# Last output tile in three pieces, a row pitch of 160 bytes, and a new order of two weight differences, in a fused attention and max-out kernel

## Chip, cores, metric

One core of a Trainium2 chip. The metric is the device time of one execution in microseconds (us); the kernel before takes 183.31 us (median of 4 runs, 183.17 to 183.59). "Span" is the profile's time from the first to the last instruction; it is some 2 us shorter than the run's time.

## The reference

Batch 4, 8 heads, 768 tokens, head width 64, cut into 8 blocks of 96 tokens. Five rounds of row and column normalisation of an 8x8 matrix per head give P; P mixes the blocks of k and v; attention stays within a block; then a max-out layer follows.

```python
k_sorted = einsum('bhij,bhjcd->bhicd', P, k_b); v_sorted = the same with v_b
attn = softmax(scale * q_b @ k_sorted^T);  x = attn @ v_sorted       # (3072, 512)
out = maximum(x @ w1, x @ w2) @ w_out                                # d_ff = 1024
```

## The kernel before

The order of issue is made by hand; tiles and their semaphores are looked after by a tile framework. max(h1, h2) is computed as relu(x(W1-W2)) plus x W2, so W1 is overwritten by W1-W2 in four quarters (`w_difference`; quarters 1 to 3 on DVE), and W2 W_out is computed once (`w2_transposes`, `w_product`). PSUM is a pool of four tiles of 128 x 1024 fp32 values.

```python
v_sb = big.tile([BLK, 128, D + 2], BF16, ...)        # sorted v, rows of 66 bf16; column 64 is ones

def values(b, u):                                     # 32 units of 8 products
    ...
    for h2 in range(2):
        for ii in range(4):
            nc.tensor.matmul(ps[:, h2*512 + ii*65 : h2*512 + (ii+1)*65], e[...],
                v_sb[:, m0 + (hp + 4*h2)*8 + ih*4 + ii, 0:65], start=True, stop=True)
    # DVE: reciprocal of the ones column's sum (rs), then the product x

def moe_out_last(ti, pieces):                         # tiles 4 and 5 of the last batch
    for n0, n1, engines in pieces:
        ps = ps_f32("out_ps")
        out_products(ps[:, 0 : n1-n0], B-1, ti, n0, n1)        # 12 products
        w = (n1 - n0) // len(engines)
        for m, eng in enumerate(engines):
            o = opool.tile([128, w], FP32, tag=f"o{n0}{m}", name="o", bufs=1)
            ...   # copy by ACT ("A") or DVE ("D"), then a store from ACT's or SP's queue
# calls: moe_out_last(4, [(0, 512, "D")]);  moe_out_last(5, [(0, 256, "A"), (256, 512, "AD")])

# batch 0, near 30 us:
    w_difference(1)
    moe_h_products(0, 0, 1, (0, 2))                   # first half of hidden unit 1
    w2_out = w2_transposes(0, "D")
    moe_h(0, 0, 0, "A", (1, 3))
    w2_out()                                          # DVE copies w2T
    SC[5]()
# then: VA[4], w_difference(2); rest of hidden unit 1; SC[6], SC[7], VA[5], w_difference(3); hidden 2 ...

# loads during batch 0, step 8:
    pair_q(1, 0), pair_q(1, 1), load_q(2), load_v(2), load_v(3)
```

The softmax here doesn't subtract the row's maximum and nothing guards it: scores larger than these inputs give would overflow.

Of the kernel before, what the change touches and what calls it, by code (L numbers as in the profile page):

```python
# [10 lines left out]
FP32 = mybir.dt.float32  # L11
BF16 = mybir.dt.bfloat16
# [3 lines left out]
def kernel(  # L16
# [16 lines left out]
    nc = tc.nc  # L33
# [4 lines left out]
    B, H, S, D = q.shape  # L38
    NB = sort_net.shape[-1]
    BLK = S // NB  # L40
# [14 lines left out]
    big = ctx.enter_context(tc.tile_pool(name="big", bufs=1))  # L55
# [4 lines left out]
    opool = ctx.enter_context(tc.tile_pool(name="opool", bufs=3))  # L60
# [4 lines left out]
    def ps_f32(name):  # L65
        return psum.tile([128, 1024], FP32, tag="ps", name=name)

    def ps_bf16(name):
        return psum.tile([128, 2048], BF16, tag="ps", name=name)
# [21 lines left out]
    def pick(a_ns, d_ns):  # L91
        if load["A"] + a_ns <= load["D"] + d_ns:
            load["A"] += a_ns
            return "A"
        load["D"] += d_ns
        return "D"

    def evac(out_ap, in_ap, n, two_x=False, eng=None):
        a_ns, d_ns = (200 + n) / 1.2, (130 + (n / 2 if two_x else n)) / 0.96
        if eng:  # L100
            load[eng] += a_ns if eng == "A" else d_ns
        if (eng or pick(a_ns, d_ns)) == "A":
            nc.scalar.copy(out=out_ap, in_=in_ap)  # L103
        else:
            nc.vector.tensor_copy(out=out_ap, in_=in_ap)  # L105
# [82 lines left out]
    def w_difference(t, eng=None):  # L188
        n = DFF // 4
        (eng or nc.vector).tensor_tensor(  # L190
            out=w1_sb[:, :, t * n : (t + 1) * n],
            in0=w1_sb[:, :, t * n : (t + 1) * n],
            in1=w2_sb[:, :, t * n : (t + 1) * n],
            op=ALU.subtract,
        )
        if not eng:
            load["D"] += 600
# [66 lines left out]
    def selections(b):  # L264
        src = ident[0:G, b * 8 : b * 8 + 8]
        if b % 2 == 0:
            sel_v[b] = const.tile([G, 16, NB], BF16, tag=f"sel_v{b}", name="sel_v")
            nc.vector.tensor_copy(
                out=sel_v[b], in_=ident[0:G, b * 8 : b * 8 + 16].to_broadcast([G, 16, NB])
            )  # L270
        sel_k[b] = const.tile([G, 8, 16], BF16, tag=f"sel_k{b}", name="sel_k")
        nc.vector.tensor_copy(out=sel_k[b], in_=src.to_broadcast([G, 8, 16]))
# [40 lines left out]
                bd_v[b] = bd_v[b + 1] = bd.rearrange("p m i -> p (m i)")  # L313


    v_sb = big.tile([BLK, 128, D + 2], BF16, tag="v_sb", name="v_sb")
    nc.vector.memset(v_sb[:, :, D : D + 1], 1.0)
    xT = big.tile([128, 2, 2, 2, 2, TCH], BF16, tag="xT", name="xT")

# [194 lines left out]
    def w2_transposes(t, eng):  # L514
        ps = ps_bf16("tw_ps")
        for n in range(16):
            fb, dmt = t * 4 + n // 4, n % 4
            nc.tensor.matmul(
                ps[:, n * 128 : (n + 1) * 128],
                w2_sb[:, dmt, fb * 128 : (fb + 1) * 128],  # L520
                ident,
                is_transpose=True,
                start=True,
                stop=True,
            )
        return lambda: evac(
            w2T[:, t * 4 : t * 4 + 4, :].rearrange("p f d -> p (f d)"),
            ps,
            2048,
            two_x=True,  # L530
            eng=eng,
        )
# [38 lines left out]
    def moe_h(b, ch, t, eng=None, hps=(0, 2, 1, 3), n=0):  # L571
        moe_h_products(b, ch, t, hps, n)
        ps = h_ps[t]
        g = gpool.tile([128, 2, TCH], BF16, tag="g", name="g")
        src = ps.rearrange("p (t f) -> p t f", t=2)[:, :, 0:TCH]
        if (eng or pick((200 + 2 * TCH) / 1.2, (130 + 2 * TCH) / 0.96)) == "A":
            nc.scalar.activation(out=g, in_=src, func=AF.Relu)  # L577
        else:
            nc.vector.tensor_scalar(  # L579
                out=g, in0=src, scalar1=0.0, scalar2=None, op0=ALU.max  # L580
            )
        g_tiles[b, ch, t] = g
# [32 lines left out]
    def moe_out_last(ti, pieces):  # L615

        tok0 = (B - 1) * S + ti * 128
        for n0, n1, engines in pieces:
            ps = ps_f32("out_ps")
            out_products(ps[:, 0 : n1 - n0], B - 1, ti, n0, n1)  # L620
            w = (n1 - n0) // len(engines)
            for m, eng in enumerate(engines):
                o = opool.tile([128, w], FP32, tag=f"o{n0}{m}", name="o", bufs=1)
                src = ps[:, m * w : (m + 1) * w]
                if eng == "A":
                    nc.scalar.copy(out=o, in_=src)
                else:
                    nc.vector.tensor_copy(out=o, in_=src)
                (nc.scalar if eng == "A" else nc.sync).dma_start(
                    out=out[tok0 : tok0 + 128, n0 + m * w : n0 + (m + 1) * w], in_=o  # L630
                )


    def att(b):
# [24 lines left out]
    SC, VA, TR = att(0)  # L659
# [22 lines left out]
    moe_h_products(0, 0, 1, (0, 2))  # L682
    for b in range(1, B):
        selections(b)
    w2_out = w2_transposes(0, "D")
    moe_h(0, 0, 0, "A", (1, 3))
    w2_out()
    SC[5]()

    def turn(rows, c0):  # L690
        turn_v(rows, "D", c0, c0 + 24)
        load["D"] += 1600

    def load_rest():
# [1 line left out]
        load_k(2)  # L696

    tail = {
        0: [VA[4], lambda: w_difference(2)],
        1: [SC[6], SC[7], VA[5], lambda: w_difference(3)],  # L700
        2: [VA[6], TR[2], VA[7]],
        3: [TR[3], lambda: w2_transposes(1, "A")(), load_rest, lambda: block_diagonals(1)],
        4: [lambda: block_diagonals(2), lambda: turn(second, 0)],
# [11 lines left out]
    for b in range(B):  # L715
        units = [lambda t=t: moe_h(b, 0, t, None if b else "A") for t in range(4)]
        if b == 0:
            units[0] = lambda: None
            units[1] = lambda: moe_h(0, 0, 1, "A", (1, 3))
        units += [lambda t=t: moe_h(b, 1, t) for t in range(4)]  # L720
        cost = [1.3] * 8
        if b == 0:
            units += [lambda dmt=dmt: w_product(dmt) for dmt in range(4)]
            cost += [1.7] * 4
        units += [
            lambda ti=ti, part=part: moe_out(b, ti, part)
            for ti in range(6 if b < B - 1 else 4)
            for part in range(2)
        ]
        cost += [1.3] * 12  # L730
        if b == B - 1:
            units += [
                lambda: moe_out_last(4, [(0, 512, "D")]),
                lambda: moe_out_last(5, [(0, 256, "A"), (256, 512, "AD")]),
            ]
        steps, lo = [], 2
        if b < B - 1:
            qs = [lambda half=half: q_transposes(b + 1, half) for half in range(2)]
            pairs = [lambda two=two: pair_q(b + 1, two) for two in range(2)]
            ks = [lambda t=t, b=b: sort_k(b + 1, t) for t in range(3)]  # L740
            SC, VA, TR = att(b + 1)

            def group(*fs):
                return [lambda: [f() for f in fs]]

            if b == 0:
                lo = 9
                tail[7] += ks
                vs = [lambda t=t: sort_v(1, t) for t in range(4)]
                for m, c in enumerate((0, 24, 48, 72)):  # L750
                    VA[m + 1 : m + 2] = group(VA[m + 1], lambda c=c: turn(both, c))
                steps = group(*vs[:3]) + qs[:1] + group(*SC[0:2], vs[3]) + qs[1:] + VA[:1]
                steps += group(*SC[2:5]) + VA[1:2]
            elif b == 1:
                vs = [lambda t=t: sort_v_pair(2, t) for t in range(8)]
                steps = group(*pairs) + group(*ks) + qs[:1] + group(*SC[0:2], vs[0]) + qs[1:]
                steps += group(*vs[1:4]) + group(*vs[4:7]) + group(*SC[2:4], vs[7]) + VA[:2]
            else:
                steps = group(*pairs) + group(*ks) + qs + group(*SC[0:2])
                steps += group(*SC[2:5]) + VA[:2]  # L760
            rest = SC[4:] if b == 1 else SC[5:]
            steps += VA[2:3] + TR[:1] + VA[3:4]
            steps += group(*rest[:-1]) + TR[1:2] + VA[4:5] + rest[-1:] + VA[5:6]
        done = 0
        for n, unit in enumerate(units):
            unit()
            for step in tail.get(n, []):
                step()
            total = sum(cost[lo:-2])
            want = -(-len(steps) * sum(cost[lo : n + 1]) // total)  # L770
            while done < min(want, len(steps)):
                steps[done]()
                done += 1
        tail = {0: [VA[6]], 1: [TR[2], VA[7]], 2: [TR[3]]}
        if b == 0:
            tail[3] = [lambda: load_k(3)]
            tail[8] = [lambda: load_q(3)]
# [28 lines left out]
```

## Time and profile before

| | before |
|---|---|
| time, median | 183.31 us |
| span of the profiled run (itself 182.86 us) | 180.8 us |
| TensorE busy | 169.9 us (94%) |
| last product's end | 176.64 us |
| span's end after that | 4.18 us |

Times in views are us from the span's start. A timeline row has start, length, engine, source line, operation, output and input; in brackets stands how long the engine had been idle and what ended that. A wait row is "who and what, waited for whom: us in total, times, longest". The busy time of TensorE in one unit of values is overlapped, so its real cost is read from the chain of waits, where each piece lasts until the next begins. In the kernel before:

```profile
146.12 0.26 PE o_ps L463 x8
150.27 0.26 PE o_ps L463 x8
```

### The profile page before, as it was taken

What the parts mean: (1) busy time and instruction counts of PE and PEld (TensorE: products, weight loads), DVE (VectorE), ACT (ScalarE), POOL (GpSimd) and SP (SyncE); (2) the same over time, 40 slices, a digit from 0 to 9 for tenths busy, and PEclk for the clock granted to TensorE, in tenths of its full rate; (3) what the DMA queues carried; (4) which work ended last, traced back from release to release, by engine and by line L of the source; (5) the groups of instructions that cost most, each with busy time, mean ns of one, the idle gap of its engine ahead of it and who ended that gap; (6) DMA issues with size and microseconds to landing.
All of it is one profiled execution on the core that took longest, in us unless ns stands there. A gap on an engine that the chain in (4) does not pass through costs nothing.

```text
span 180.8 us, 4625 instructions
## 1 busy us (share of the span) xinstructions
PE 169.9 (94%) x2071; PEld 100.7 (56%) x2071; DVE 93.9 (52%) x192; ACT 92.0 (51%) x110; POOL 22.9 (13%) x39
## 2 busy tenths in 40 slices
PE   7698999999999999999989999999999999999990
PEld 2246666656655544577655554667555456554460
DVE  5878495759863595164587343446344427222010
ACT  3696776777665445277783341575815213530011
POOL 7941533200280000001000000000000000000000
PEclk9999999999999999999999999999999999999999
DMA  4999999999199992037400302300003032000341
GB/s 71 198 201 205 201 207 218 198 204 211 23 133 218 208 251 96 30 120 107 71 4 0 120 0 116 120 0 5 0 4 116 0 120 116 0 4 0 116 172 60
DMA packets 13939, 19.17 MB, mean 106 GB/s; under 512 B 800, under 2 KB 8864, under 8 KB 13920
## 3 DMA queue, kind: packets, MB, share of 16 engines
q0 software_dynamic: 10304, 12.58, 41.2%
q1 hardware_dynamic: 3328, 6.10, 8.8%
q8 instruction: 16, 0.26, 0.6%
q10 hardware_dynamic: 288, 0.20, 0.3%
q14 instruction: 3, 0.02, 0.0%
HBM read 25.17 MB, written 6.29 MB: 174 GB/s over the span
## 4 chain that ended last, share of the span: by engine, by line
PE 61%; DMA 22%; DVE 6%; issue 4%; POOL 3%; ACT 1%; ACTq 0%; POOLq 0%; DVEq 0%
PE out_ps L590 30%; PE h_ps L563 17%; DMA q_raw<-in_q_dram 15%; DMA v_raw<-in_v_dram 6%; PE o_ps L463 3%; PE tx_ps L495 3%; PE s_ps L438 2%; DVE x L480 2%; PE k_ps L371 2%; DVE g L579 2%; PE tq_ps L341 1%; PE v_ps L392 1%; POOL v_raw L153 1%; DMA out_dram<-o 1%; DVE xT L105 1%
## 5 line engine op out<-in xcount | busy, mean ns | idle before, releaser
L590 PE MATMUL out_ps<-wo_sb,g 128*128 128x512 bf16 (+1 forms) x200 | 47.9, 371 | 0.2 <-DVE g L579 0.2
L563 PE MATMUL h_ps<-xT,w_sb 128*128 128x384 bf16 x256 | 46.3, 326 | 0.6 <-DVE g L579 0.2
L563 PEld LDWEIGHTS <-w_sb 128*128 128x128 bf16 x256 | 23.6, 98 | 15.2 <-issue 0.5
L577 ACT ACTIVATE g<-h_ps 128x768 bf16<-128x768 f32 x24 | 19.5, 811 | 23.6 <-PE h_ps L563 23.6
L446 ACT ACTIVATE e<-s_ps 96x768 bf16<-96x768 f32 x32 | 24.1, 803 | 13.7 <-PE s_ps L438 13.6
L590 PEld LDWEIGHTS <-g 128*128 128x128 bf16 x200 | 17.5, 97 | 15.8 <-issue 0.2
L590 PE MATMUL out_ps<-wc,xT 128*128 128x512 bf16 (+1 forms) x100 | 24.8, 370 | 0.0
L103 ACT COPY o<-out_ps 128x1024 f32<-128x1024 f32 x8 | 8.1, 1013 | 31.1 <-PE out_ps L590 27.4
L480 DVE TENSOR_TENSOR x<-o_ps,rs 96x512 bf16<-96x512 f32 x32 | 22.0, 687 | 1.1
L474 DVE RECIPROCAL rs<-o_ps 96x8 f32<-96x8 f32 x32 | 6.4, 200 | 27.3 <-PE o_ps L463 27.2
L590 PEld LDWEIGHTS <-xT 128*128 128x128 bf16 x100 | 9.8, 98 | 11.0
L463 PEld LDWEIGHTS <-e 96*128 96x128 bf16 x256 | 11.5, 98 | 6.1 <-DVE x L480 0.7
L209 DVE COPY v_dc<-v_raw 64x1536 bf16<-64x1536 bf16 (+2 forms) x9 | 14.1, 1584 | 1.4 <-DMA v_raw<-in_v_dram 1.4
L579 DVE TENSOR_SCALAR g<-h_ps 128x768 bf16<-128x768 f32 x8 | 7.7, 958 | 13.5 <-PE h_ps L563 10.6
L463 PE MATMUL o_ps<-v_sb,e 96*128 96x65 bf16 x256 | 13.3, 194 | 1.0 <-DVE w2T L105 0.4
L105 DVE CAST v_sb<-v_ps 96x1024 bf16<-96x1024 f32 x7 | 8.5, 1218 | 5.9 <-PE v_ps L392 3.9
L103 ACT CAST v_sb<-v_ps 96x1024 bf16<-96x1024 f32 x9 | 8.7, 1018 | 3.3 <-PE v_ps L392 2.5
L103 ACT CAST kT<-k_ps 128x1024 bf16<-128x1024 f32 x10 | 9.5, 1024 | 0.0
L103 ACT COPY xT<-tx_ps 128x768 bf16<-128x768 bf16 x11 | 8.8, 797 | 1.5 <-PE tx_ps L495 1.5
L438 PEld LDWEIGHTS <-kT 64*128 64x128 bf16 x256 | 6.1, 94 | 5.5 <-issue 4.6
L129 POOL DMA_DIRECT2D q_raw<-in_q_dram x4 | 3.6, 900 | 43.3 <-DVE q_pair L326 41.0
L495 PEld LDWEIGHTS <-x 96*128 96x128 bf16 x128 | 6.8, 97 | 3.7 <-DVE x L480 1.7
(78 smaller groups left out, 163.9 us busy)
## 6 DMA issues: line engine op xcount, KB each, us to landing
out_dram<-o SPq DMA_DIRECT2D x11, 512.0 KB, 2.8
k_raw<-in_k_dram POOLq DMA_DIRECT2D x12, 256.0 KB, 13.4
q_raw<-in_q_dram POOLq DMA_DIRECT2D x4, 768.0 KB, 8.8
v_raw<-in_v_dram POOLq DMA_DIRECT2D x6, 384.0 KB, 11.6
w_sb<-in_moe_w_dram POOLq DMA_DIRECT2D x3, 512.0 KB, 16.1
wo_sb<-in_moe_w_out_dram POOLq DMA_DIRECT2D x2, 512.0 KB, 20.0
v_raw<-in_v_dram POOLq DMA_DIRECT2D x3, 256.0 KB, 4.5
w_sb<-in_moe_w_dram POOLq DMA_DIRECT2D x2, 256.0 KB, 14.1
```

Of the source, the lines that this page charges most:

```text
L103: nc.scalar.copy(out=out_ap, in_=in_ap)
L105: nc.vector.tensor_copy(out=out_ap, in_=in_ap)
L209: nc.vector.tensor_copy(out=dst, in_=src)
L438: nc.tensor.matmul(ps[:, h2 * 512 + ii * BLK : h2 * 512 + (ii + 1) * BLK], kT[b][rows, (hp * 8 + i) * BLK : (hp * 8 + i) * BLK + 128], rhs ...
L446: nc.scalar.activation(out=e[:, 0 : 8 * BLK].rearrange("p (t f) -> p t f", t=2), in_=ps[0:BLK].rearrange("p (t f) -> p t f", t=2)[:, :, 0 ...
L463: nc.tensor.matmul(ps[:, h2 * 512 + ii * 65 : h2 * 512 + (ii + 1) * 65], e[:, (h2 * 4 + ii) * BLK : (h2 * 4 + ii) * BLK + 128], v_sb[:, m0 ...
L480: nc.vector.tensor_tensor(out=x, in0=ov[:, :, :, 0:D], in1=rs.to_broadcast([BLK, 2, 4, D]), op=ALU.mult,)
L495: nc.tensor.matmul(ps[:, h2 * 1024 + ii * BLK : h2 * 1024 + (ii + 1) * BLK], x[:, h2, ii].rearrange("p n d -> p (n d)"), ident[0:BLK, 0:BL ...
L563: nc.tensor.matmul(h_ps[t][:, m * 512 : m * 512 + TCH], w1_sb[:, hp, fb * 128 : (fb + 1) * 128], xT[:, b % 2, ch, hp % 2, hp // 2, :], sta ...
L577: nc.scalar.activation(out=g, in_=src, func=AF.Relu)
L579: nc.vector.tensor_scalar(out=g, in0=src, scalar1=0.0, scalar2=None, op0=ALU.max)
L590: nc.tensor.matmul(dst, g_tiles[b, ch, m // 2][:, m % 2, off : off + 128] if m < NFB else xT[:, b % 2, ch, hp % 2, hp // 2, off : off + 12 ...
```

## The change

Intent: let the last stores leave sooner, put the rows of v_sb on multiples of 32 bytes, and fill DVE's idle times near 30 us so that TensorE doesn't wait there.

```diff
-    v_sb = big.tile([BLK, 128, D + 2], BF16, tag="v_sb", name="v_sb")
+    v_sb = big.tile([BLK, 128, D + 16], BF16, tag="v_sb", name="v_sb")
 ...
-            w = (n1 - n0) // len(engines)
-            for m, eng in enumerate(engines):
-                o = opool.tile([128, w], FP32, tag=f"o{n0}{m}", name="o", bufs=1)
+            o = opool.tile([128, n1 - n0], FP32, tag=f"o{ti}{n0}", name="o", bufs=1)
 ...   (copy and store as before, one engine per piece)
+    w_difference(2)
     w2_out = w2_transposes(0, "D")
     moe_h(0, 0, 0, "A", (1, 3))
     w2_out()
+    w_difference(3)
+    moe_h(0, 0, 1, "A", (1, 3))
     SC[5]()
 ...   (the three are taken out of their later places)
-                lambda: moe_out_last(5, [(0, 256, "A"), (256, 512, "AD")]),
+                lambda: moe_out_last(5, [(0, 256, "A"), (256, 384, "D"), (384, 512, "A")]),
```

More of the change, by code (lines that the diff above doesn't have):

```diff
@@ L617, in moe_out_last @@
         tok0 = (B - 1) * S + ti * 128
-        for n0, n1, engines in pieces:
+        for n0, n1, eng in pieces:
             ps = ps_f32("out_ps")
             out_products(ps[:, 0 : n1 - n0], B - 1, ti, n0, n1)
-            w = (n1 - n0) // len(engines)
-            for m, eng in enumerate(engines):
-                o = opool.tile([128, w], FP32, tag=f"o{n0}{m}", name="o", bufs=1)
-                src = ps[:, m * w : (m + 1) * w]
-                if eng == "A":
-                    nc.scalar.copy(out=o, in_=src)
-                else:
-                    nc.vector.tensor_copy(out=o, in_=src)
-                (nc.scalar if eng == "A" else nc.sync).dma_start(
-                    out=out[tok0 : tok0 + 128, n0 + m * w : n0 + (m + 1) * w], in_=o
-                )
+            o = opool.tile([128, n1 - n0], FP32, tag=f"o{ti}{n0}", name="o", bufs=1)
+            if eng == "A":
+                nc.scalar.copy(out=o, in_=ps[:, 0 : n1 - n0])
+            else:
+                nc.vector.tensor_copy(out=o, in_=ps[:, 0 : n1 - n0])
+            (nc.scalar if eng == "A" else nc.sync).dma_start(
+                out=out[tok0 : tok0 + 128, n0:n1], in_=o
+            )
     def att(b):
@@ L698 @@
     tail = {
-        0: [VA[4], lambda: w_difference(2)],
-        1: [SC[6], SC[7], VA[5], lambda: w_difference(3)],
+        0: [VA[4]],
+        1: [SC[6], SC[7], VA[5]],
         2: [VA[6], TR[2], VA[7]],
@@ L718 @@
             units[0] = lambda: None
-            units[1] = lambda: moe_h(0, 0, 1, "A", (1, 3))
+            units[1] = lambda: None
         units += [lambda t=t: moe_h(b, 1, t) for t in range(4)]
```

## The prediction

> **What bounds the kernel now.** I read the page first. Its table of busy time and its slices say that TensorE is the engine to watch, at full granted clock from end to end, and that the last slice is the one stretch where it stands still.
>
> ```profile
> PE 169.9 (94%) x2071; PEld 100.7 (56%) x2071; DVE 93.9 (52%) x192; ACT 92.0 (51%) x110; POOL 22.9 (13%) x39
> ...
> PE   7698999999999999999989999999999999999990
> ```
>
> So a change pays where it shortens TensorE's own list of work, one of its waits, or the stretch after its last product. I looked at those three in turn. The end first: the timeline of the last microseconds.
>
> ```profile
> 174.06 0.69 DVE L628 COPY o<-out_ps 128x512 f32<-128x512 f32 x1 [6.49 <-PE out_ps L590]
> ...
> 174.78 3.91 SPq L629 DMA_DIRECT2D out_dram<-o  x2
> ...
> 175.17 1.04 PE L590 MATMUL out_ps<-wo_sb,g 128*128 128x256 bf16 x8
> ...
> 176.04 0.60 PE L590 MATMUL out_ps<-wc,xT 128*128 128x256 bf16 x4
> 176.90 0.37 ACT L626 COPY o<-out_ps 128x256 f32<-128x256 f32 x1 [4.38 <-DMA out_dram<-o]
> 177.31 0.37 ACTq L629 DMA_DIRECT2D out_dram<-o  x1
> 177.72 0.27 ACT L626 COPY o<-out_ps 128x128 f32<-128x128 f32 x1 [0.45 <-ACT o L626]
> 178.02 0.34 ACTq L629 DMA_DIRECT2D out_dram<-o  x1
> 178.02 0.29 DVE L628 COPY o<-out_ps 128x128 f32<-128x128 f32 x1 [3.27 <-ACT o L626]
> ```
>
> The products are through at 176.64, but the span ends at 180.82: 4.18 us without a product. Three pieces queue in it. The copy of the first piece could have begun at 175.33, when its twelve products end, yet it waits to 176.90 for a transfer. The code says which: tile 4 and the first piece of tile 5 share one SBUF tag, so ACT must wait until the store of tile 4 has landed. Then ACT makes two copies with an issue between, and DVE's copy stands behind ACT's, because both read the same PSUM tile. DVE's store, issued at about 178.34, is the last to land.
>
> Second, the waits in the middle: the table of waits by pair, and TensorE's timeline around 30 us.
>
> ```profile
> POOL q_raw L129 <- DVE q_pair L326: 41.0, 2, 27.7
> ...
> DVE v_dc L209 <- DMA v_raw<-in_v_dram: 1.4, 1, 1.4
> ```
>
> ```profile
> 29.84 0.41 PE L463 MATMUL o_ps<-v_sb,e 96*128 96x65 bf16 x8 [0.39 <-DVE w2T L105]
> ...
> 31.87 1.47 PE L563 MATMUL h_ps<-xT,w_sb 128*128 128x384 bf16 x8 [0.16 <-DVE w_sb L190]
> ...
> 34.24 1.46 PE L563 MATMUL h_ps<-xT,w_sb 128*128 128x384 bf16 x8
> 64.11 0.43 PE L463 MATMUL o_ps<-v_sb,e 96*128 96x65 bf16 x8 [0.23 <-DVE x L480]
> ```
>
> The two waits on DVE near 30 us are what the reordering aims at. The wait at 64.11 shows what bounds the stretch before it: DVE there had waited for a load of v that landed at 61.60, and this load was issued once DVE had made q_pair, at 48.7. A gain on TensorE alone between 49 and 64 us is therefore lost at 64.11; a gain that also lets DVE finish earlier at 48.7 is kept.
>
> Third, the products that read v_sb: thirty-two units of eight, 0.26 us each.
>
> ```profile
> L463 PE MATMUL o_ps<-v_sb,e x256: 190/193/204, 22.1 to 152.2; 96*128 96x65 bf16 x128
> ```
>
> **What the Trainium skill says.** "SBUF — State Buffer", section "Door 1: The DMA port swizzle", says that SBUF has lines of 16 bytes and that crossing to a new one costs. A row of v_sb is 66 bf16 values, 132 bytes, so of every four neighbouring rows only one starts on such a line. The trace fits: within a unit the eight products start, for example, 35, 32, 33, 32, 29, 33, 32 and 33 ns apart (at 114.45 us), and in every unit it is the fifth product, one that starts on a line, that takes 29 or 30 ns. "TensorE: Matmul & The Clock Gate", section "Wait — 56ns, not 53.3ns?", gives N/2.4 ns plus 2.5 ns between products of N columns: 29.6 ns for 65. The trace agrees for aligned operands: 56, 109, 162 and 216 ns at 128, 256, 384 and 512 columns, weights loaded each time. "PSUM — Partial Sum Buffer", section "PSUM bank collisions raise a hardware error", says that two engines must not read one bank together, so such copies are put in sequence; the DVE copy at 178.02, just after ACT's ended at 178.00, shows it. "DMA: Bandwidth & Descriptors", section "Anatomy of one DMA", gives a fixed cost near 2 us; here the three last stores took 1.6 to 1.7 us from issue to landing.
>
> **Part 1, the last tile.** Removed: the wait for tile 4's store, and DVE's wait for ACT. Added: twelve products more, since 12 of 256 columns become 24 of 128.
> - TensorE: 12 x 109 ns = 1.31 us becomes 24 x 56 ns = 1.34 us (the 56 ns from the transposes of W2, 128 columns with a weight load each). The second half starts at 175.17; the second piece is issued from 175.17 to 175.84, the third from 175.84. The last product starts at 176.46 and with 0.22 us of length ends at 176.68.
> - First piece: ACT copies from 175.35 (0.37), issues by 176.14. It is out of the way.
> - Second piece: DVE copies from about 176.05 (0.29), SP issues at 176.36, landing 1.6 later, at 178.0.
> - Third piece: ACT copies from 176.70, 0.28 to 176.98; issue at 177.00; landing 1.62 later (as ACT's last store had it: 178.02 to 179.64), at 178.62.
> - Before, the last landing was 179.92 and the span ended 0.90 later. The same 0.90 now gives 179.52. **Gain 1.30 us**, all of it at the end of the chain.
>
> **Part 2, the pitch of 160 bytes.** Every row of v_sb now starts on a multiple of 32 bytes. In a unit six products (all but the first, which carries the start of the group, and the fifth) go from about 32.5 to 29.3 ns: 6 x 3.2 = 19 ns, and for 32 units 0.61 us. Not all of it shows. Eight units stand before 35 us, mostly beside waits on other engines, and three between 49 and 61 us, where the gain is lost at 64.11. Of the 21 from 64.11 on, those next to the three waits of 0.4 to 0.5 us (118.4, 130.1 and 154.05 us) can be half hidden. I take 18 x 19 ns: **gain 0.35 us**. The copies into v_sb cost the same as the other copies of 1024 columns (1018 against 1024 ns on ACT, 1220 against 1226 on DVE), so I expect nothing there.
>
> **Part 3, the order near 30 us.** No work is added; the built program shows that W1-W2 of quarters 2 and 3 now stands around the copy of w2T on DVE, and that the second half of the hidden unit 1 comes before scores 5 on TensorE, and its activation before that of scores 5 on ACT. By the durations of before:
> - DVE: the quarter-2 difference 27.30 to 27.98 (its weights landed at 26.94), w2T still 28.56 to 29.79, quarter 3 to 30.48.
> - TensorE: hidden unit 1 from 29.01 to 29.66, scores 5 to 30.0, values 4 at 30.05 (w2T is done, the 0.45 us wait is gone), scores 6 at 30.4.
> - ACT: g of unit 0 at 29.21, g of unit 1 at 29.92, e of scores 5 at 30.63 to 31.44 (steps of 0.71 us, as in the trace). Scores 7 needs the buffer of unit 1, free at 30.73; values 5 needs e of scores 5, so it starts at 31.49 instead of 31.29. This is a wait that takes the place of the removed one.
> - The hidden unit 2 then starts at 31.76 instead of 31.87, and unit 3, which waits for the activation of unit 2 in both, at 34.13 instead of 34.24.
> **Gain 0.10 us**, and it is passed on, as DVE's row to 48.7 starts from TensorE's results.
>
> Sum: 1.30 + 0.35 + 0.10 = 1.75 us; the median of 183.26 becomes **181.5 us**, 1.0% less.
>
> **Rivals.**
> - The fifth product is fast because it is the first in its PSUM bank, not because of its row: it is also the first of the second head. For it: both hold in all 32 units. Against it: 29.6 ns is the rate of all other products here, so the others are the odd ones, and PSUM's position does not single them out (the third and the fifth are both on 8 bytes there, and the third takes 32 or 33). Then part 2 gives nothing: 181.85 us.
> - Weight loads bind the narrow products of the last pieces: a load is recorded at 98 ns, and 24 of them in a row would need 2.35 us instead of 1.34. Against it: the 16 transposes start 56 ns apart with a load each. Then the end gains 0.3 us only: 182.5 us.
> - ACT becomes the bound near 30 us by more than I worked out (it has g, g, e, e, e and g in a row), or the second difference delays w2T if its load lands late (margin 0.35 us). That costs some 0.3 us: 181.9 us.
> - Part 3's gain, and more of part 2's, is swallowed by the load that ends at 61.60: 181.6 us.
>
> **Range and chances.** Part 1 is sure within 0.2 us, as each of its terms is a duration of the same kind measured in the same stretch. Parts 2 and 3 together may give from -0.2 to 0.75 us. With 0.1 us of spread between runs that is 180.9 to 182.1 us. To be faster by over 2% it would have to be under 179.6, for which I see no term: 0.02. Slower by over 2%: 0.01. Within 2%: 0.97.
>
> **What would show it.** In the changed profile: the copy of the first piece at about 175.35 less the earlier gains (0.45 us), with no transfer before it; DVE's last copy ahead of ACT's last; about 2.8 us from the last product to the span's end instead of 4.18; 0.24 us for a unit of values, with its inner starts all 29 or 30 ns apart; no wait on w2T or w_sb near 30 us but one on ACT before values 5; the wait near 64 us unchanged or grown. I am wrong if the span still ends 4 us after the last product, if the pieces of 128 columns go out slower than 60 ns apart, or if values keep 0.26 us.

## More of the kernel before

One caution: the chain of waits of the kernel before puts 14.8% on the load of q_raw and shows no DVE between 44 and 49 us. The table of waits says that the load issued at 48.74 had waited for DVE's q_pair. A chain follows one releaser per step; a second view is needed before its largest entry is believed.

## The result, and the profile after

The changed kernel takes **181.61 us** (median of 4 runs, 181.56 to 181.95) against 183.31: ratio 0.9909, 95% interval 0.9892 to 0.9926. All ratios here are the mean of one kernel's runs over the mean of the other's of the same rounds, so not quite the ratio of the medians quoted. Executions in which one die ran at a lower clock are left out of the means. The profiled run of the kernel before was a quick one (182.86 us), so the two spans (180.8 and 179.5) differ by only 1.3 us; gains are better read inside the traces, from one event to another.

The end, timeline of the changed kernel:

```profile
174.10 0.69 DVE L625 COPY o<-out_ps 128x512 f32<-128x512 f32 x1 [6.49 <-PE out_ps L590]
...
175.21 0.61 PE L590 MATMUL out_ps<-wo_sb,g 128*128 128x128 bf16 x8
175.41 0.37 ACT L623 COPY o<-out_ps 128x256 f32<-128x256 f32 x1 [2.84 <-PE out_ps L590]
...
175.88 0.61 PE L590 MATMUL out_ps<-wo_sb,g 128*128 128x128 bf16 x8
176.08 0.29 DVE L625 COPY o<-out_ps 128x128 f32<-128x128 f32 x1 [1.29 <-PE out_ps L590]
...
176.32 0.39 PE L590 MATMUL out_ps<-wc,xT 128*128 128x128 bf16 x4
176.75 0.27 ACT L623 COPY o<-out_ps 128x128 f32<-128x128 f32 x1 [0.97 <-PE out_ps L590]
177.04 0.34 ACTq L626 DMA_DIRECT2D out_dram<-o  x1
```

All three copies now wait for nothing but their products, DVE's runs ahead of ACT's second one, and twelve products of 128 columns take 175.88 - 175.21 = 0.67 us, 56 ns each. From the last product's end (176.71) to the span's end (179.51) there are 2.80 us, where there were 4.18.

Near 30 us and near 64 us, TensorE's rows in the same view, and the values units in the chain of waits:

```profile
30.14 0.42 PE L463 MATMUL o_ps<-v_sb,e 96*128 96x65 bf16 x8
...
31.57 0.42 PE L463 MATMUL o_ps<-v_sb,e 96*128 96x65 bf16 x8 [0.35 <-ACT e L446]
31.83 1.46 PE L563 MATMUL h_ps<-xT,w_sb 128*128 128x384 bf16 x8
...
64.39 0.42 PE L463 MATMUL o_ps<-v_sb,e 96*128 96x65 bf16 x8 [0.60 <-DVE x L480]
```

```profile
146.19 0.24 PE o_ps L463 x8
150.32 0.24 PE o_ps L463 x8
```

The two waits on DVE near 30 us are gone, and one on ACT (e of scores 5) has come. Near 64 us the wait has grown from 0.23 to 0.60 us of idle time. This is why the last products of the two traces end nearly together (176.64 and 176.71) although a unit of values went from 0.26 to 0.24 us: TensorE came to this point sooner (the group before it starts at 62.33, against 62.42), and the load of v held it back: the third of its four parts, for which DVE waited, landed at 61.88 instead of 61.60.

### The profile page after: what moved, and what is told of

Same layout as the page of the kernel before. It is cut to its first block, busy times and chain, and to the rows that moved or that the text cites. A ratio compares the mean times of both kernels' runs of the same rounds, so it can differ in the third digit from the quotient of the medians.

```text
span 179.5 us, 4648 instructions
## 1 busy us (share of the span) xinstructions
PE 170.0 (95%) x2083; PEld 100.7 (56%) x2083; DVE 94.0 (52%) x192; ACT 91.8 (51%) x110; POOL 22.9 (13%) x39
## 4 chain that ended last, share of the span: by engine, by line
PE 58%; DMA 29%; DVE 5%; issue 4%; POOL 2%; ACT 1%; POOLq 0%; DVEq 0%
PE out_ps L590 32%; PE h_ps L563 16%; DMA v_raw<-in_v_dram 10%; DMA w_sb<-in_moe_w_dram 10%; DMA q_raw<-in_q_dram 9%; PE o_ps L463 3%; PE tx_ps L495 2%; PE k_ps L371 2%; PE s_ps L438 2%; DVE g L579 2%; PE tq_ps L341 1%; DVE x L480 1%; DVE xT L105 1%; POOL v_raw L153 1%; DVE v_dc L209 1%
## 5 line engine op out<-in xcount | busy, mean ns | idle before, releaser
L590 PE MATMUL out_ps<-wo_sb,g 128*128 128x512 bf16 (+2 forms) x208 | 48.1, 363 | 0.2 <-DVE g L579 0.2
L590 PE MATMUL out_ps<-wc,xT 128*128 128x512 bf16 (+2 forms) x104 | 25.0, 362 | 0.0
L463 PE MATMUL o_ps<-v_sb,e 96*128 96x65 bf16 x256 | 12.9, 193 | 1.3 <-DVE x L480 0.6
L438 PE MATMUL s_ps<-qT,kT 64*128 64x96 bf16 x256 | 9.0, 204 | 0.1
## 6 DMA issues: line engine op xcount, KB each, us to landing
k_raw<-in_k_dram POOLq DMA_DIRECT2D x12, 256.0 KB, 13.7
```

Of the source, the lines that this page charges most:

```text
L438: nc.tensor.matmul(ps[:, h2 * 512 + ii * BLK : h2 * 512 + (ii + 1) * BLK], kT[b][rows, (hp * 8 + i) * BLK : (hp * 8 + i) * BLK + 128], rhs ...
L463: nc.tensor.matmul(ps[:, h2 * 512 + ii * 65 : h2 * 512 + (ii + 1) * 65], e[:, (h2 * 4 + ii) * BLK : (h2 * 4 + ii) * BLK + 128], v_sb[:, m0 ...
L590: nc.tensor.matmul(dst, g_tiles[b, ch, m // 2][:, m % 2, off : off + 128] if m < NFB else xT[:, b % 2, ch, hp % 2, hp // 2, off : off + 12 ...
```

## The experiments

Twelve experiments were run: ten other kernels, and the changed kernel twice more. All outputs are right. "The kernel before" of each group of runs is that of the same chip and rounds: 183.61 us in the first two groups, 183.51 in the third; the last kernel (`row_orders`) ran once, beside one run of the kernel before (183.60).

**The three parts alone.** Each is the kernel before with one part of the diff above; the fourth is the changed kernel again.

> The kernel before with part 1 alone (three pieces with their own PSUM and SBUF tiles). My theory, the end of the chain: the span's end comes 2.8 us after the last product instead of 4.18, so 1.3 to 1.4 us less than the kernel before, ratio 0.9926 to 0.993. Rival, that parts 2 and 3 carry a good part of the gain of 1.7 us: less than 1.0 us here.

Measured: 182.22 us, ratio 0.9924 (0.9911 to 0.9937), 1.39 us less than 183.61. The span ends 2.80 us after the last product. Part 1 is most of the gain.

> The kernel before with the pitch of 160 bytes alone. My theory: each unit of eight products that reads v_sb goes from 0.258 to 0.244 us, 14 ns less rather than the 19 ns of the prediction, and only the 21 units after the load of v that ends near 61.6 us count, so 0.2 to 0.3 us less, ratio 0.9984 to 0.9989. Rival, that all 32 units count: 0.45 us, ratio 0.9975. Rival, that the pitch is worth nothing by itself: 1.000.

Measured: 183.34 us, ratio 0.9987 (0.9975 to 0.9999), 0.27 us less. The traces give a sharper figure. From the start of the values unit held up by the load of v to the last product's end, the kernel before needs 176.64 - 64.11 = 112.53 us and the run with part 3 alone 112.54; the run with part 2 alone needs 112.28. With part 1 in both, it is 112.57 without the pitch and 112.32 with it. The pitch is worth **0.25 us** after that point, in both pairs. The units, averaged over those whole in the trace after 64 us, went from 258.7 to 245.4 ns.

> The kernel before with the order near 30 us alone. My theory of the prediction: 0.1 us less, ratio 0.9995, as waits on DVE of 0.45 and 0.23 us give way to waits on ACT of 0.2 and 0.5 us. Rival, that what is gained before 61.6 us is all lost in the wait for the load of v: 1.000 and a longer wait before the values near 64 us. Rival, that it does harm: over 1.0005.

Measured: 183.31 us, ratio 0.9987 (0.9975 to 0.9999), 0.30 us less by the medians, with an interval nearly as wide as the gain. In the trace, from the first values unit to hidden unit 3 there are 12.10 us in the kernel before (22.14 to 34.24) and 11.96 here (22.04 to 34.00), **0.14 us** less. From there to the issue of the load of q that goes ahead of v, both need 14.5 us, so the gain is handed on to the load (issued at 48.48, not 48.74). But the part of v that DVE waits for landed at 61.93, later than in the kernel before (61.60), and TensorE waited longer:

```profile
31.37 0.43 PE L463 MATMUL o_ps<-v_sb,e 96*128 96x65 bf16 x8 [0.35 <-ACT e L446]
...
64.46 0.43 PE L463 MATMUL o_ps<-v_sb,e 96*128 96x65 bf16 x8 [0.83 <-DVE x L480]
```

From the issue of the load of q to the landing of this part of v it took 12.9 to 13.7 us in the first six profiles. That scatter of 0.8 us is several times what part 3 gains, so one run cannot tell whether the gain arrives; see the last experiment.

> The changed kernel again, on the chip of its three parts. If the parts add: its difference to the kernel before is the sum of the three differences within 0.15 us, 1.6 to 1.8 us, ratio 0.990 to 0.9913.

Measured: 181.81 us, ratio 0.990 (0.9887 to 0.9912), 1.80 us less. The three alone sum to 1.39 + 0.27 + 0.30 = 1.96, 0.16 more than that, a hair over the 0.15 us allowed and inside the intervals of the small parts (0.2 us each way). So the parts add, as far as these runs can tell.

**Which half of part 1.**

```diff
# tag_only: the kernel before, with
-                o = opool.tile([128, w], FP32, tag=f"o{n0}{m}", name="o", bufs=1)
+                o = opool.tile([128, w], FP32, tag=f"o{ti}{n0}{m}", name="o", bufs=1)
# psum_only: part 1 alone, with
-            o = opool.tile([128, n1 - n0], FP32, tag=f"o{ti}{n0}", name="o", bufs=1)
+            o = opool.tile([128, n1 - n0], FP32, tag=f"o{n0}", name="o", bufs=1)
```

> The kernel before, but the first piece of tile 5 has an SBUF tile of its own; the other half stays one PSUM tile read by ACT and then by DVE. My theory: ACT's first copy comes 1.5 us sooner, DVE's last copy at about 0.34 us after the last product's end and the span's end 3.2 us after the last product instead of 4.2. So 1.0 us less than the kernel before, ratio 0.9945. Rival, that the shared PSUM tile is the main cost of the end: less than 0.4 us.

Measured: 182.59 us, ratio 0.9945 (0.9933 to 0.9957), 1.02 us less; the span ends 3.13 us after the last product. Timeline of its end, in which ACT's first copy now waits for its products alone:

```profile
176.09 0.37 ACT L626 COPY o<-out_ps 128x256 f32<-128x256 f32 x1 [2.84 <-PE out_ps L590]
...
176.76 0.60 PE L590 MATMUL out_ps<-wc,xT 128*128 128x256 bf16 x4
177.40 0.27 ACT L626 COPY o<-out_ps 128x128 f32<-128x128 f32 x1 [0.94 <-PE out_ps L590]
177.69 0.34 ACTq L629 DMA_DIRECT2D out_dram<-o  x1
177.69 0.29 DVE L628 COPY o<-out_ps 128x128 f32<-128x128 f32 x1 [2.23 <-ACT o L626]
```

> The kernel before with three pieces, each with its own PSUM tile, but with the SBUF tile of the first piece shared with tile 4 as before. My theory: ACT's first copy still waits for the store of tile 4, its second copy and store follow, and the end comes 3.9 us after the last product: 0.3 us less than the kernel before, ratio 0.9984. Rival (shared PSUM tile is the main cost): 1.0 us less. In neither case does this and the run with the tag alone add to the whole part 1 by chance: 0.3 + 1.0 = 1.3 against the 1.39 measured.

Measured: 183.16 us, ratio 0.9981 (0.9963 to 0.9998; one of six runs took 184.13), 0.45 us less by the medians; the span ends 3.79 us after the last product. Timeline of its end:

```profile
176.96 0.39 PE L590 MATMUL out_ps<-wc,xT 128*128 128x128 bf16 x4
...
177.57 0.37 ACT L623 COPY o<-out_ps 128x256 f32<-128x256 f32 x1 [4.37 <-DMA out_dram<-o]
177.97 0.38 ACTq L626 DMA_DIRECT2D out_dram<-o  x1
178.39 0.27 ACT L623 COPY o<-out_ps 128x128 f32<-128x128 f32 x1 [0.45 <-ACT o L623]
```

With the PSUM tile still shared, DVE's copy (0.29) stays behind ACT's: 3.13 - 2.80 = 0.33 us of loss. With the SBUF tile still shared, ACT's first copy waits for the store of tile 4: 3.79 - 2.80 = 0.99 us. So about three quarters of part 1 is the name of a buffer, and a quarter the third PSUM tile.

**Why the pitch helps.** The prediction held that a row is slow when it doesn't start on a line of 16 bytes.

```diff
# pitch_144: the changed kernel, with
-    v_sb = big.tile([BLK, 128, D + 16], BF16, tag="v_sb", name="v_sb")
+    v_sb = big.tile([BLK, 128, D + 8], BF16, tag="v_sb", name="v_sb")
# pitch_160_shifted: the changed kernel, with each row's 65 values in columns 2 to 66, e.g.
-                    v_sb[:, m0 + (hp + 4 * h2) * 8 + ih * 4 + ii, 0:65],
+                    v_sb[:, m0 + (hp + 4 * h2) * 8 + ih * 4 + ii, 2:67],
```

> The changed kernel with a pitch of 144 bytes: rows start on multiples of 16 bytes, every other one off a multiple of 32. My theory (the start on a line of 16 bytes counts): the same as the changed kernel, 244 ns per unit, ratio 0.990. Rival (multiples of 32 bytes count): every other product takes 32 or 33 ns, about 250 ns per unit, 0.12 us more than the changed kernel.

Measured: 181.64 us, ratio 0.9896 (0.9883 to 0.9909); 245.1 ns per unit, as with 160 bytes.

> The changed kernel, pitch 160 bytes, but the 65 values of a row start 4 bytes into it, so no row starts on a line. My theory: all eight products of a unit take 32 or 33 ns, 262 ns per unit, also the fifth, which took 29 in the kernel before: 0.35 to 0.4 us more than the changed kernel, ratio 0.992. Rival (the fifth is fast as first in its PSUM bank, and the pitch is what counts): the fifth stays at 29, or all stay at 29 to 30 and the time is that of the changed kernel, 0.990.

Measured: 181.75 us, ratio 0.9897 (0.9883 to 0.991); 242.0 ns per unit, not slower at all. The explanation of the prediction falls: with no row on a line, the products are as quick as with every row on one. The rival of the bank falls too, since here and in the changed kernel the second to fourth products, in the same bank as the first, are quick. What differs from the kernel before is the gap between rows. A row of 130 bytes at a pitch of 132 ends 2 bytes before the next begins, so three of four neighbouring rows begin in the very line of 16 bytes in which the last one ended; with gaps of 14 or 30 bytes here, none does. (This takes v_sb itself to start on a line. The traces don't give its address, but in every unit of the kernel before the second to fourth products are slow, and this rule then needs a start on a line or 2 bytes past one; both give the same pattern.) The new theory was put to its own test, two layouts and three reading orders in one kernel:

```diff
# row_orders: the changed kernel, with
+    for pair, pitch in ((0, D + 2), (1, D + 4)):     # 132 bytes for batches 0, 1; 136 for 2, 3
+        v_by[pair] = big.tile([BLK, 128, pitch], BF16, tag=f"v_sb{pair}", name="v_sb")
 ...
+        if ih == 1:         order = [(h2, ii) for ii in range(4) for h2 in range(2)]
+        elif hp % 2 == 0:   order = [(h2, ii) for h2 in range(2) for ii in range(4)]
+        else:               order = [(h2, ii) for h2 in range(2) for ii in (3, 2, 1, 0)]
```

> A look at start times, not at the total. The pitch is 132 bytes for batches 0 and 1 and 136 bytes for 2 and 3; in the first half of a batch's units the rows are read upwards in even units and downwards in odd ones, in the second half the two heads take turns, so that no product reads a row next to the one just read. The run with shifted rows showed that a start off a line of 16 bytes costs nothing by itself. New theory: a product is slow (32 to 33 ns) when it begins in the line of 16 bytes in which the product before it ended. Then, at 132 bytes: upwards the second to fourth and sixth to eighth are slow, as before; taking turns all are 29 to 30 (but for the start of the unit and one odd value of 33 to 35). At 136 bytes: upwards only every other one is slow (second, fourth, sixth, eighth), taking turns none. Downwards tells whether a line shared with the start of the product before is slow too. Rival (where a row starts counts after all): the order makes no difference, and the taking of turns stays at 32 to 33. Rival (the pitch as such): all products of both layouts stay slow.

Measured, one look (182.04 us, one run at a granted clock of 1.0; one run can't tell its state, so its time is not used): time in ns from each product's start to the next one's, one unit of each kind, from the trace's start times.

```
pitch  order        at us    1   2   3   4   5   6   7   8
132    upwards       55.4   34  33  33  32  30  33  32  33
132    downwards     59.1   34  30  29  29  33  29  30  29
132    taking turns  33.3   34  29  30  29  32  29  30  29
136    upwards       99.3   34  32  30  32  29  33  29  33
136    downwards    102.5   34  30  29  29  32  30  29  29
136    taking turns 107.7   34  29  32  29  29  30  32  29
for comparison, the kernel before, the changed kernel, and the shifted rows:
132    upwards      107.1   34  32  33  32  30  32  33  32
160    upwards      107.2   34  29  30  29  29  35  29  29
160+4  upwards      107.6   34  29  29  29  29  33  29  29
```

This is the pattern that was written down beforehand, but for one miss: at 136 bytes, taking turns should have left no odd value, and it leaves two, at the third and the seventh product. At 132 bytes upwards all neighbours are slow; at 136 bytes (gap 6) only every other one is, namely those whose beginning falls into the line where the row before ended; turned round or taken in turns, the same bytes at the same pitch are quick. A line of 32 bytes would have made all neighbours at 136 slow and half of those at 144; one of 8 bytes, none at 136. Turning the order round also turns the order of the columns in PSUM, but that is not the cause: read upwards, all pitches write the same columns, and only 132 and 136 are slow. Reading downwards, where a product ends in the line in which the one before began, costs nothing. One or two odd values of 32 to 35 ns are left in every quick unit, and what causes them is not settled. With them, products 2 to 8 of a unit average 30.3 ns in the changed kernel and 29.8 with the shifted rows, against 32.2 in the kernel before (units after 64 us).

**The load of v.** In the changed kernel, three loads were put in another order:

```diff
# v_first: the changed kernel, with
-            lambda: load_q(2),
             lambda: load_v(2),
             lambda: load_v(3),
+            lambda: load_q(2),
# v_first_old_order: the same, with part 3 undone
```

> The changed kernel with the loads of v for batches 2 and 3 issued ahead of the load of q for batch 2. My theory, that the wait of the values near 64 us for this load bounds the first third: the load lands by 58 us, DVE's wait for it and TensorE's wait of 0.7 to 1.1 us before the values near 64 us are gone, and the time is 0.7 to 1.0 us less than the changed kernel, 1.35 to 1.5% less than the kernel before (ratio 0.985 to 0.9865). Rival, that the wait only looks like the bound and another (ACT, or the load of q) takes its place: within 0.3 us of the changed kernel.

Measured: **180.45 us**, ratio 0.9834 (0.982 to 0.9848) to the kernel before, and 1.25 us less than the changed kernel's 181.70 in the same rounds. The loads of v start at 36.6 us (batch 2) and 44.5 us (batch 3), as they need not wait for q_pair; the last part lands at 54.3. In the table of waits the changed kernel of these rounds has the first line below; here it is gone, and the load of v waits for DVE instead, where that costs nothing:

```profile
DVE v_dc L209 <- DMA v_raw<-in_v_dram: 1.7, 1, 1.7
```

```profile
POOL v_raw L153 <- DVE v_dc L209: 8.2, 2, 6.6
```

The timeline of TensorE has the unit of values without a wait:

```profile
63.27 0.41 PE L463 MATMUL o_ps<-v_sb,e 96*128 96x65 bf16 x8
```

The gain is a little above the expectation. Counted from start to start, beyond the rate of the products (the idle time in the views is about 0.16 us shorter, as it begins at a product's modelled end), the wait before these values was 0.77 us in the changed kernel of this group; and of the 1.27 us by which the last product ends sooner, 0.50 was there when the first values unit began (at 21.90 us, against 22.40). The moved loads are not issued before 36.6 us, so this is scatter: that unit starts between 21.90 and 22.41 us in the fourteen traces. So 0.77 us is accounted for by the wait, which was 0.76 to 1.16 us in the changed kernel's three traces (1.00 and 1.02 with `pitch_144` and `pitch_160_shifted`); whether the rest of 1.25 us is chance is open.

> The same with part 3 undone. My theory: with the load out of the way nothing swallows what part 3 gains, 0.1 to 0.2 us, so this is 0.1 to 0.2 us slower than the run with the loads of v first. Rival, that part 3 gives nothing or harms: equal or faster.

Measured: 180.50 us, ratio 0.984 (0.9826 to 0.9854), 0.05 us more than with part 3: too little for these intervals. In the traces, counted from the scores that follow the first values unit (at 22.25 and 22.47), the hidden unit 3 comes at 33.84 and 34.21, and the last product ends at 175.58 and 175.95. The start accounts for 0.22 of both differences of about 0.37, so part 3 gains 0.15 us by 34 us and 0.14 still at the end. With the load out of the way its gain is kept.

> The changed kernel on the same chip as these two, to compare with: ratio 0.990 as in the two measurements so far, and its wait before the values near 64 us again 0.7 us or more.

Measured: 181.70 us, ratio 0.9912 (0.9897 to 0.9927), with the wait of 0.77 us.

## Why the prediction was right, and where it was not

- **The whole**: 181.5 us predicted, 181.61 measured, well in the range. That the sum came so near is partly luck: part 1 gave 0.08 us more and part 2 gave 0.10 less than said, and the wait for the load of v, whose length is in no term of the sum, was 0.76 to 1.16 us in three traces of the changed kernel. The upper end of the range was also set too low for its own terms: 1.10 for part 1 and -0.2 for the rest would leave 182.36 us, not 182.1.
- **What bounds the kernel**: right. The end is bound by its copies and stores, and the load of v near 62 us cuts the kernel in two; moving that load by itself shows it (`v_first`).
- **Part 1**: the step from the last product to the end was put at 179.52 - 176.68 = 2.84 us, and is 2.80. It was worth 1.39 us alone by time, and 4.18 - 2.80 = 1.38 from the last product to the end, where 1.30 was predicted. (One reading was a little off: the last three stores of the kernel before took 1.58 to 1.75 us to land, not 1.6 to 1.7.) The rival of weight loads binding the narrow products fell: 56 ns each.
- **Part 2**: the step that failed is the reason, "of every four neighbouring rows only one starts on such a line". Where a row starts made no difference in these runs; what counts is that it begins in the line in which the one just read ended. The prediction's reason and the measured one single out the same products at a pitch of 132 bytes, which is why the number came out near, by luck and not by the mechanism: 13 ns per unit instead of 19, since each quick unit keeps an odd value of 33 to 35 ns, so 0.25 us instead of 0.35. The fifth product is quick because the product before it reads a row far away, not because its own row starts on a line.
- **Part 3**: right in kind and size (0.14 to 0.15 us in the traces, 0.10 predicted), down to the wait on ACT that replaces those on DVE. That it "is passed on" was true as far as the load's issue; beyond it the scatter of the load hides it, and only `v_first` and its partner show it at the end. By time alone it is not separated from zero by much (0.9987, at most 0.9999).
- **The wait near 64 us**: foreseen as "unchanged or grown", and it grew. The expected shift of the end copies by 0.45 us did not come in the profiled pair, because the load landed 0.28 us later there.

## What to carry to other kernels

Read the end of a kernel from the last product on, instruction by instruction: here a shared buffer name alone cost 1.0 us. Before counting a gain, find the next transfer that TensorE must meet; what is gained ahead of it only lengthens the wait, and reordering the loads (1.25 us by time, 0.77 of it explained) was then worth about three quarters of what the whole change gave. And when a layout change helps, vary the reading order as well as the layout: the first explanation that fits the numbers may name the wrong one of two things that move together.

## What the Trainium skill lacked or had wrong

- "SBUF — State Buffer", section "Door 1: The DMA port swizzle", says that each access crossing to a new line of 16 bytes pays. For TensorE's moving operand the runs show another rule, which no page has: a product of 65 bf16 columns takes 32 to 33 ns from start to start instead of 29 to 30 when it begins in the 16-byte line in which the product before it ended (132 bytes: three of four; 136: every other; 144 and 160: none), and a start 4 bytes into a line costs nothing (242 ns per unit against 245).
- "TensorE: Matmul & The Clock Gate", section "Back-to-back issue gap", gives 81 ns for products of 128 columns in a stream with weight loads and 131 ns for 512. Here they start 56 and 216 ns apart, a weight load each, which is the rate that the page calls isolated.
- "DMA: Bandwidth & Descriptors", section "Anatomy of one DMA", has a fixed cost of about 2.0 us, but for DMAs issued by GpSimd, not from the queues of ACT and SP that these stores use. The store of 64 KB from ACT's queue lands 1.57 us after its issue (177.04 to 178.61), which is shorter.
- No page says how much a group of loads varies: from the issue of the load of q to the landing of the third of the four loads of v behind it took 12.9 to 13.7 us in six profiles.
